# Q and K of two units by halves, and the end of the softmax as one lump for seven groups of heads, in a kernel of two attention layers

## The chip, the cores and the metric

The kernel runs on one core of a Trainium2 chip. The metric is the device time of one execution in microseconds (us), as the median of several runs. Inputs and outputs are in fp32, and each matrix product is made of three matmuls on fp32r parts of the numbers.

## The reference: two attention layers side by side

Two layers, A and B, have inputs of their own: x of 2048 positions by 1024, a weight for Q, K and V (1024 by 3072) and an output weight (1024 by 1024); 32 heads of 32. Their outputs stand side by side. In layer A a position sees 8 keys, each two positions apart; in layer B it sees the 256 keys up to itself.

```
# layer A
off = jnp.arange(8) * 2
idx = pos[:, None] - off[None, :]
logits = jnp.einsum("bhsd,bhswd->bhsw", q, kg) * scale      # kg, vg: k, v gathered at idx
attn = _softmax(jnp.where(mask[None, None, :, :], logits, -1e9))
o = jnp.einsum("bhsw,bhswd->bhsd", attn, vg)
# layer B
mask = (idx[:, None] - idx[None, :] >= 0) & (idx[:, None] - idx[None, :] < 256)
# both: out = o.reshape(B, S, D) @ wo; concatenate([a, b], axis=-1)
```

## The kernel before

The work is cut into 8 units of 512 positions: units 0 to 3 are layer B, units 4 to 7 layer A. In layer A the even and the odd positions are two sequences of 1024, so that the 8 keys are neighbours, and units 4 and 5 are one of them, 6 and 7 the other. Each unit has 8 groups of four heads; group hg = 8 x unit + group, so 32 to 63 are layer A's.

A host-side planner writes the whole program. The list `plan` gives the pieces of matrix products in order: "qk" (Q and K of one group), "v", "vp" (values), "o" and "p" (output products). Each becomes a list of items, one item being three matmuls (`TERMS`: high by high, high by low, low by high) for one of eight slices k of the contraction. Beside this sequence, "g", stand the sequences of the attention: the scores and the values of each group. A model of all engines, `Clock` (`ck`), gives each item a time from which it may start; the loop at the end emits the item that the model says is ready first. `ck.defer(t, f)` puts a follow-up step into a list of later steps that is emitted, in order of modelled time, among the others. So the order in which the steps stand on an engine comes out of modelled times, and a change in one place can move others.

Weights and x come as raw fp32 by DMAs that GpSimd issues (L221). Each is split in two fp32r parts: the high part by a cast on ScalarE (L276) or VectorE (L279), the low part by a subtraction on VectorE (L282). The x of a unit comes in four DMAs of two slices each.

All matmuls stand at L324. PSUM has three banks in a ring for matrix products (tag g), four for scores (s), one for values (o). An item with k = 0 takes a bank; the copy that empties it gives it back. Q and K are emptied on ScalarE (L586, L591), values' projections by a copy into vbuf (L720), output products on VectorE (L902) or ScalarE (L925).

A group of layer A goes through `window`: 128 small matmuls for the scores of four heads, mask on VectorE (L1217), maximum (L1227), subtraction (L1229), exponential on ScalarE (L1233), sum (L1241) and reciprocal (L1243), then `scale` (L1247) and `turn`, a transpose (L1254), each deferred to the modelled end of the step before it; `spread` writes the result into the block-diagonal `wide` by eight copies on ScalarE (L1263, L1266). The values' matmuls (o<-wide,vbuf) follow, are copied out at L1336 and stored to DRAM through od. In units 4 to 7 the sums that VectorE makes of blocks of the weights and outputs for products with fewer multiplications stand at L1104 and L1136.

In the tables of the profile PE is TensorE, PEld its weight loads, DVE VectorE, ACT ScalarE, POOL GpSimd and SP SyncE.

Of the kernel before, what the change touches and what calls it, by code (L numbers as in the profile page):

```python
# [16 lines left out]
NK = 8  # L17
# [13 lines left out]
EXTRA, EACH = 246, 5.2  # L31
P_LATE = 1.5
PAIRED = 50
VPARTS = ((0,4),(4,2),(6,2))
V_SLOTS = {0:0,5:1,7:2}
O_SLOTS = {2: (0, 1), 3: (2, 3), 4: (4, 5), 5: (6, 7)}
# [255 lines left out]
def kernel(ctx, tc, xs, wqk, wv, wo, outs, units):  # L292
# [3 lines left out]
    U = len(units)  # L296
    DU = sum(u[2] for u in units)
# [18 lines left out]
    ck = Clock()  # L316
# [98 lines left out]
    for p in plan:  # L415
# [7 lines left out]
        elif p[0] == "v":  # L423
            s0, n = VPARTS[p[2]]
            for i, g in enumerate((0, 1) if n == 2 else (0, 1, 2, 3, 0)):
# [97 lines left out]
    pfree = [0.0]  # L523
    vbuf = [const.tile([P, 6, n * P], F32, name=f"vbuf{i}") for i, (_, n) in enumerate(VPARTS)]
    vpart = {s0 + i: (p, i * P) for p, (s0, n) in enumerate(VPARTS) for i in range(n)}
    tails = const.tile([P, NG, 8], F32, name="tails")
# [37 lines left out]
    def latest(*ts):  # L564
        return None if any(t is None for t in ts) else max(ts)
# [162 lines left out]
    def v_items(u, part):  # L728
# [4 lines left out]
        h = {"w": {}}  # L733
        s0, ng = VPARTS[part]
        wide = ng == 4
# [330 lines left out]
    def value_load(part):  # L1066

        u = VPAIR + 1
        s0, n = VPARTS[part]
        if (u, part) in done["v"] or len(done["vd"]) < 4 or \  # L1070
# [94 lines left out]
    def x_items(u):  # L1165
        xt[u], xready[u] = [], []

        def run(g):
            a, b = st.get(where["x", u, g])
            xt[u] += a  # L1170
            xready[u] += b

        return [[(lambda: 0.0, lambda g=g: run(g), 0.0, lambda: None)] for g in range(4)]


    def window(u, s):
# [4 lines left out]
        hg = u * NG + s  # L1181
# [6 lines left out]
        def p16():  # L1188
            return band[buf][:, :1024].rearrange("p (i c) -> p i c", c=64)[:, :, 24:]
# [3 lines left out]
        h = {}  # L1193

        def scores_ready():
            if last_dense + 1 < hg < PAIRED and hg - 1 not in done["p"]:
                return None
            return latest(rs.empty(), done["stack"].get((u, s)), done["p"][hg - 1] + P_LATE if last_dense + 1 < hg < PAIRED else 0.0,
                          done["clear"].get(buf) if hg - 2 <= last_dense else done["o"].get(hg - 2))
# [25 lines left out]
        def top():  # L1225
            nm = small.tile([P, 16], F32, tag="nm", name="nm")
            nc.vector.tensor_reduce(nm, p16(), axis=mybir.AxisListType.X, op=ALU.max)  # L1227
            ck.use("dve", 0.855, ck.now)
            nc.vector.tensor_tensor(p16(), p16(), nm[:, :, None].to_broadcast([P, 16, 40]), op=ALU.subtract)  # L1229
            e = ck.use("dve", 0.86, ck.now, port=True)  # L1230

            def expo():
                nc.scalar.activation(p16(), p16(), AF.Exp)  # L1233
                e2 = ck.use("act", 0.645, e)
                ck.defer(e2 - 0.1, lambda: total(e2))

            ck.defer(e - 0.1, expo)

        def total(e):
            sm = small.tile([P, 16], F32, tag="sm", name="sm")  # L1240
            nc.vector.tensor_reduce(sm, p16(), axis=mybir.AxisListType.X, op=ALU.add)  # L1241
            ck.use("dve", 0.855, e)
            nc.vector.reciprocal(sm, sm)  # L1243
            e = ck.use("dve", 0.285, ck.now)

            def scale():
                nc.vector.tensor_tensor(p16(), p16(), sm[:, :, None].to_broadcast([P, 16, 40]), op=ALU.mult)  # L1247
                e = ck.use("dve", 0.86, ck.now, port=True)
                ck.defer(e - 0.1, turn)

            ck.defer(e - 0.1, scale)

        def turn():
            nc.vector.transpose(band[buf][:, 1024:], band[buf][:, :1024])  # L1254
# [14 lines left out]
        def values_ready():  # L1269
            if hg + 1 < PAIRED and hg + 1 not in done["scores"]:  # L1270
                return None
            return latest(done["v"].get((u, vp)), h.get("p") and h["p"] + P_LATE, ro.when())
# [14 lines left out]

        return [Item(scores_ready, scores, CW, 256 + (16 * len(kbs) if hg < PAIRED else 0))], [Item(values_ready, values, C3 + 0.9, 16 * len(kbs))]

# [260 lines left out]
    def fill(at, n):  # L1550

        def run():
            mm(ps, idle[:, :P], idle, start=True, stop=True)

        def after(last):
            if last:
                rs.give(bank, ck.now + ck.SEM)

        return [(lambda: 0.0, run, CG, lambda i=i: after(at == FILL[-1][0] and i == n - 1)) for i in range(n)]
# [10 lines left out]
    for p in plan:  # L1570
        if not marks and p[1:] == (DU, 2) and p[0] == "qk":
            marks.append(len(gemm))
        if len(marks) == 1 and p[0] == "p":
            marks.append(len(gemm))
        if p[0] == "qk":
            new = qk_items(p[1], p[2])
            if p == ("qk", 0, 0):
                q, k, x = new[:NK], new[NK:], x_items(0)
                f = dict(FILL)
                new = x[0] + sum([q[i:i + 1] + fill(i + 1, f.get(i + 1, 0)) for i in range(4)], [])  # L1580
                for i in (1, 2, 3):
                    new[new.index(q[2 * i]) if i < 2 else len(new):0] = x[i]
                    if i == 1:
                        new += k[:4]
                    else:
                        new += q[2 * i:2 * i + 2] + k[2 * i:2 * i + 2]
            if p[1:] == (0, NG - 1):
                x1 = x1 or x_items(1)
                for g in range(3, FIRST_X - 1, -1):
                    new[NK + 2 * g - 2:NK + 2 * g - 2] = x1[g]  # L1590
            gemm += new
        elif p[0] == "v":
            new = v_items(p[1], p[2])
            if p[1:] == (0, 2) and FIRST_X:
                x1 = x_items(1)
                for g in range(FIRST_X - 1, -1, -1):
                    new[X1_AT[g]:X1_AT[g]] = x1[g]
            elif V_SLOTS.get(NG - 1) == p[2] and 0 < p[1] < U - 1:
                m = 2 * VPARTS[p[2]][1]
                for g, x in reversed(list(enumerate(x_items(p[1] + 1)))):  # L1600
                    new[m * g + XAT:m * g + XAT] = x
            gemm += new
        elif p[0] == "o":
            gemm += o_items(p[1], p[2])
        elif p[0] == "p":
            gemm += product(p[1], p[2])
        elif p[0] == "vp":
            new = value_product(p[2])
            if VP_AT.get((p[1], NG - 1)) == p[2:] and p[1] + 1 < U:
                for g, x in reversed(list(enumerate(x_items(p[1] + 1)))):  # L1610
                    new[4 * g + XAT:4 * g + XAT] = x
            gemm += new
# [87 lines left out]
```

## The time and profile before

| | |
|---|---|
| median of 3 runs | 1789.3 us (1788.56 to 1789.42) |
| profiled execution | 1788.09 us, span 1786.4 us |
| granted TensorE clock | 1.000 |
| PE busy | 1768.4 us (99%) |
| DVE busy | 1295.5 us (73%) |
| ACT busy | 936.9 us (52%) |
| POOL busy | 412.8 us (23%) |
| instructions | 38443 |

The span runs from the first to the last instruction of the profiled execution; its device time is 1.7 us longer. The busy share of an engine is an average over the program. Rows of the timeline give the start, the busy time, the engine, the line, the operation with output <- input, the number of instructions in the row, and in brackets the idle time ahead of it and what ended it.

### The profile page before, as it was taken

The numbers are of one execution on the slowest core, as the hardware profiler recorded it, in microseconds if no ns is written. First come the engines' busy times: TensorE is split into PE (matmuls) and PEld (weight loads), VectorE is DVE, ScalarE is ACT, GpSimd is POOL, SyncE is SP. The second block draws the span as 40 slices with busy tenths as digits, with TensorE's granted clock in tenths as the row PEclk, the third lists the DMA queues.
The fourth block names the chain that finished last, engine by engine and source line by source line (L and its number), as shares of the span: only waits on it lengthen the run. The fifth ranks groups of instructions, "written<-read, shape, count | busy, mean of one in ns | idle before, by whom it ended". The sixth has DMA issues, their size and how long they took to land.

```text
span 1786.4 us, 38443 instructions
## 1 busy us (share of the span) xinstructions
PE 1768.4 (99%) x14496; PEld 1440.2 (81%) x14496; DVE 1295.5 (73%) x2881; ACT 936.9 (52%) x2332; POOL 412.8 (23%) x962
## 2 busy tenths in 40 slices
PE   9999999999999999999999999999999999999999
PEld 7787778888777888778788788878888887877887
DVE  6777876768867769867669546566577868767866
ACT  5565566555656565655654524444354546455442
POOL 3322324222333233242323410110011101001210
PEclk9999999999999999999999999999999999999999
DMA  8354664645645556555556255656576758948984
GB/s 256 106 151 136 187 167 137 163 135 152 186 142 154 154 127 173 150 148 156 133 142 186 72 181 180 210 193 209 175 219 197 233 169 290 303 151 271 310 319 144
DMA packets 154793, 324.57 MB, mean 182 GB/s; under 512 B 18032, under 2 KB 58992, under 8 KB 154608
## 3 DMA queue, kind: packets, MB, share of 16 engines
q0 software_dynamic: 45792, 166.74, 30.3%
q1 hardware_dynamic: 98736, 137.02, 26.9%
q10 hardware_dynamic: 10080, 18.35, 2.8%
q8 instruction: 115, 1.88, 0.4%
q14 instruction: 70, 0.57, 0.1%
HBM read 201.33 MB, written 53.48 MB: 143 GB/s over the span
## 4 chain that ended last, share of the span: by engine, by line
PE 92%; DVE 2%; DMA 2%; ACT 2%; issue 1%; SPq 0%; ACTq 0%; DVEq 0%; POOLq 0%
PE g L324 72%; PE s L324 13%; PE o L324 7%; DMA raw<-xs 1%; DVE w L282 1%; ACT s L1403 0%; DMA raw<-sd 0%; DMA pbuf<-nat 0%; DMA raw<-wqk 0%; DVE x L282 0%; ACT w L276 0%; DMA raw<-sx 0%; DMA qst<-nat 0%; ACT wide L1263 0%; ACT x L276 0%
## 5 line engine op out<-in xcount | busy, mean ns | idle before, releaser
L324 PE MATMUL g<-x,w 128*128 128x512 f32 x3552 | 875.8, 393 | 2.9 <-ACT x L276 1.0
L324 PEld LDWEIGHTS g<-x,w 128*128 128x128 f32 x3552 | 655.9, 188 | 131.7 <-issue 6.6
L282 DVE TENSOR_TENSOR w<-raw,w 128x512 fp32r<-128x512 f32 x510 | 334.3, 697 | 53.5 <-ACT w L276 47.2
L1398 DVE CUSTOM_DVE_ANT_0 s<-s,mask_d 128x384 f32<-128x384 f32 (+2 forms) x512 | 261.8, 554 | 98.4 <-PE s L324 98.1
L1403 ACT ACTIVATE s<-s,nm 128x384 f32<-128x384 f32 (+2 forms) x512 | 274.3, 537 | 109.9 <-DVE nm L1398 103.3
L324 PE MATMUL g<-w,x 128*128 128x256 f32 (+1 forms) x1728 | 306.9, 327 | 0.9 <-DVE w L282 0.7
L1462 POOL TENSOR_SCALAR_AFFINE_SELECT pbuf<-pbuf 128x128 f32<-128x128 f32 (+1 forms) x605 | 220.1, 392 | 315.7 <-ACT pbuf L1483 313.6
L324 PEld LDWEIGHTS g<-w,x 128*128 128x128 f32 x1728 | 255.3, 190 | 26.3 <-DVE w L282 2.2
L324 PE MATMUL g<-r,w 128*128 128x512 f32 x960 | 238.4, 393 | 0.5 <-DVE r L1362 0.5
L1483 ACT ACTIVATE pbuf<-s 128x384 f32<-128x384 f32 (+2 forms) x480 | 203.4, 504 | 65.3 <-PE s L324 63.5
L324 PEld LDWEIGHTS g<-r,w 128*128 128x128 f32 x960 | 177.2, 188 | 36.0 <-DVE r L1362 1.1
L221 POOL DMA_DIRECT2D raw<-wqk x126 | 68.4, 543 | 388.9 <-DVE w L282 265.2
L324 PEld LDWEIGHTS s<-qst,kst 128*128 128x128 f32 x704 | 113.5, 188 | 42.2 <-ACT s L1403 16.9
L324 PE MATMUL s<-kst,qst 96*128 96x384 f32 (+2 forms) x512 | 142.2, 342 | 0.9 <-ACT s L1403 0.7
L324 PE MATMUL s<-qst,kst 128*128 128x256 f32 (+2 forms) x704 | 137.0, 301 | 4.0 <-ACT s L1403 3.2
L279 DVE CAST w<-raw 128x1024 fp32r<-128x1024 f32 x176 | 121.3, 689 | 8.8 <-PE g L324 7.9
L324 PEld LDWEIGHTS s<-kst,qst 96*128 96x128 f32 x512 | 93.6, 189 | 26.2 <-issue 4.5
L276 ACT CAST w<-raw 128x1024 fp32r<-128x1024 f32 (+1 forms) x80 | 82.4, 1037 | 51.7 <-PE g L324 16.0
L1403 ACT ACTIVATION_READ_ACCUMULATOR s<-s,nm 128x1 f32 x512 | 105.3, 206 | 0.0
L1263 ACT COPY wide<-band 32x512 f32<-32x512 f32 x128 | 79.0, 617 | 30.3 <-DVE band L1254 28.8
L324 PE MATMUL o<-pbuf,vbuf 128*32 128x384 f32 (+2 forms) x1408 | 91.1, 388 | 0.0
L625 ACT ACTIVATE nat<-g 128x512 fp32r<-128x512 f32 x64 | 38.3, 598 | 97.7 <-PE g L324 87.1
(90 smaller groups left out, 1426.6 us busy)
## 6 DMA issues: line engine op xcount, KB each, us to landing
raw<-wqk POOLq DMA_DIRECT2D x126, 512.0 KB, 4.6
raw<-wv POOLq DMA_DIRECT2D x60, 512.0 KB, 4.8
qst<-nat SPq DMA_DIRECT2D x96, 256.0 KB, 4.2
kst<-nat SPq DMA_DIRECT2D x96, 256.0 KB, 5.5
raw<-wo POOLq DMA_DIRECT2D x44, 512.0 KB, 4.4
raw<-xs POOLq DMA_DIRECT2D x28, 512.0 KB, 4.5
kst<-halo SPq DMA_DIRECT2D x72, 128.0 KB, 4.5
pbuf<-nat SPq DMA_DIRECT2D x128, 65.0 KB, 3.2
```

The lines of the kernel that those rows point to most:

```text
L221: (self.nc.scalar if early else self.nc.gpsimd).dma_start(raw if len(ap.shape) == 2 else raw.rearrange("p (a b) -> p a b", a=2), ap)
L276: nc.scalar.copy(t[:, 0, :], raw)
L279: nc.vector.tensor_copy(t[:, 0, :], raw)
L282: nc.vector.tensor_tensor(t[:, 1, c:c + 512], raw[:, c:c + 512], t[:, 0, c:c + 512].bitcast(F32), op=ALU.subtract)
L324: nc.tensor.matmul(out, left, right, **k)
L625: nc.scalar.activation(hl[:, 0, :], ps, AF.Copy, scale=sc)
L1263: nc.scalar.copy(diag[r:r + 32, :, :, c:c + 32], turned[r:r + 32, :, :, 1, :])
L1398: nc.vector.tensor_tensor_reduce(ps[:, :n], ps[:, :n], mask[:, cut:full], scale=-1.0, scalar=BIG, op0=ALU.add, op1=ALU.min, accum_out=nm)
L1403: nc.scalar.activation(ps[:, :n], ps[:, :n], AF.Exp, bias=nm, scale=-1.0, accum_out=sm)
L1462: nc.gpsimd.affine_select(w, w, pattern=[[0, m], [step, n]], compare_op=ALU.is_ge, fill=0.0, base=base, channel_multiplier=chan)
L1483: nc.scalar.activation(w, ps[:, :pack * n].rearrange("p (j n) -> p j n", j=pack), AF.Exp)
```

## The change

Two things are changed. First, in `window` a new function `step` replaces the two `ck.defer` calls for `scale` and `turn`: for groups below `LUMPS` = 57 it defers as before, for groups 57 to 63 (unit 7 without its first group) it emits the step at once. Reciprocal, scale and transpose of these groups then stand directly behind each other on VectorE. Second, for the first group of units 5 and 6 the items of "qk" are put in another order: Q's slices 0 to 3, K's 0 to 3, Q's 4 to 7, K's 4 to 7. Before, all eight of Q came first. Q and K then have a bank open at the same time. (The first unit of layer A is unit 4, `DU`.) In the changed file the lines up to the new function stand one number lower down, those from `turn` on seven (L1247 becomes L1248, L1254 L1261).

```
--- before.py
+++ after.py
@@ -31,6 +31,7 @@
 EXTRA, EACH = 246, 5.2
 P_LATE = 1.5
 PAIRED = 50
+LUMPS = 57
 VPARTS = ((0,4),(4,2),(6,2))
 V_SLOTS = {0:0,5:1,7:2}
 O_SLOTS = {2: (0, 1), 3: (2, 3), 4: (4, 5), 5: (6, 7)}
@@ -1246,9 +1247,15 @@
             def scale():
                 nc.vector.tensor_tensor(p16(), p16(), sm[:, :, None].to_broadcast([P, 16, 40]), op=ALU.mult)
                 e = ck.use("dve", 0.86, ck.now, port=True)
-                ck.defer(e - 0.1, turn)
-
-            ck.defer(e - 0.1, scale)
+                step(e, turn)
+
+            step(e, scale)
+
+        def step(e, f):
+            if hg < LUMPS:
+                ck.defer(e - 0.1, f)
+            else:
+                f()
 
         def turn():
             nc.vector.transpose(band[buf][:, 1024:], band[buf][:, :1024])
@@ -1584,6 +1591,8 @@
                         new += k[:4]
                     else:
                         new += q[2 * i:2 * i + 2] + k[2 * i:2 * i + 2]
+            if DU < p[1] < U - 1 and p[2] == 0:
+                new = [new[c + i] for h in (0, NK // 2) for c in (0, NK) for i in range(h, h + NK // 2)]
             if p[1:] == (0, NG - 1):
                 x1 = x1 or x_items(1)
                 for g in range(3, FIRST_X - 1, -1):
```

Where instructions move, three places. In the rows, a name's number tells one buffer from another; "waits" names the semaphores that the instruction waits for. First TensorE at Q and K of unit 5: g_12557 is Q's bank, x_12418 to x_12532 are the eight slices of x, w_12414 and w_12488 the weights of Q and K. Before (the end of Q and the start of K, whose bank is g_12590):

```order
L324 MATMUL g_12557<-x_12529,w_12414 128x512 [waits Activation_49]
L324 MATMUL g_12557<-x_12529,w_12414 128x512 [waits DVE_49]
L324 MATMUL g_12557<-x_12529,w_12414 128x512
L324 MATMUL g_12557<-x_12532,w_12414 128x512 [waits Activation_49]
L324 MATMUL g_12557<-x_12532,w_12414 128x512 [waits DVE_49]
L324 MATMUL g_12557<-x_12532,w_12414 128x512
L324 MATMUL g_12590<-x_12418,w_12488 128x512 [waits Activation_49]
L324 MATMUL g_12590<-x_12418,w_12488 128x512 x2
L324 MATMUL g_12590<-x_12421,w_12488 128x512 x3
L324 MATMUL g_12590<-x_12454,w_12488 128x512 x3
L324 MATMUL g_12590<-x_12457,w_12488 128x512 x3
```

Now (K's bank is g_12574):

```order
L325 MATMUL g_12557<-x_12457,w_12414 128x512 [waits Activation_49]
L325 MATMUL g_12557<-x_12457,w_12414 128x512 [waits DVE_49]
L325 MATMUL g_12557<-x_12457,w_12414 128x512
L325 MATMUL g_12574<-x_12418,w_12488 128x512 [waits Activation_49]
L325 MATMUL g_12574<-x_12418,w_12488 128x512
L325 MATMUL g_12574<-x_12418,w_12488 128x512 [waits DVE_49]
L325 MATMUL g_12574<-x_12421,w_12488 128x512 x3
L325 MATMUL g_12574<-x_12454,w_12488 128x512 x3
L325 MATMUL g_12574<-x_12457,w_12488 128x512 x3
L325 MATMUL g_12557<-x_12492,w_12414 128x512
L325 MATMUL g_12557<-x_12492,w_12414 128x512 [waits DVE_49]
L325 MATMUL g_12557<-x_12492,w_12414 128x512
```

K's first four slices have moved ahead of Q's last four, and the matmuls of Q behind them have lost their wait for ScalarE, which stands at K's first matmul. In unit 6 the same move takes place.

Second, ScalarE at the same place: x_12529 and x_12532 are the last two slices of x, g_12402 and g_12424 the two banks of unit 4's last values. Before:

```order
L276 CAST x_12529<-raw_12523 128x512 [waits DMASW4_49,PE_49]
L276 CAST x_12532<-raw_12523 128x512 [waits PE_49]
L720 COPY vbuf2_129<-g_12402 128x512 [waits PE_49]
L720 COPY vbuf2_129<-g_12424 128x512 [waits PE_49]
L586 ACTIVATE nat_12588<-g_12557 128x512 [waits DMAHW4_49,DMAHW3_49,DMAHW5_49,DMAHW2_49,DMAHW6_49,DMAHW1_49,DMAHW7_49,DMAHW0_49,PE_49]
L1263 COPY wide_10858<-band_10856 32x16x32 [waits DVE_49]
```

Now:

```order
L277 CAST x_12529<-raw_12523 128x512 [waits DMASW4_49,PE_49]
L277 CAST x_12532<-raw_12523 128x512 [waits PE_49]
L721 COPY vbuf2_129<-g_12402 128x512 [waits PE_49]
L721 COPY vbuf2_129<-g_12424 128x512 [waits PE_49]
L277 CAST w_12586<-raw_12555 128x1024 [waits DMASW5_49,DVE_49]
L1270 COPY wide_10858<-band_10856 32x16x32 [waits DVE_49]
```

The casts and the two copies stand as they did; behind them the cast of a weight of V has come in from VectorE, and Q's L587 copy (L586 before) has moved behind the copies into wide.

Third, VectorE and ScalarE at the end of the softmax of group 62, whose buffer is band_10856. VectorE before, from the sum to the scale (the transpose stands seven rows further down):

```order
L1241 TENSOR_REDUCE sm_18594<-band_10856 128x16 [waits Activation_49]
L1243 RECIPROCAL sm_18594<-sm_18594 128x16 [waits DVE_49]
L282 TENSOR_TENSOR x_18622<-raw_18620,x_18622 128x512 [waits DMASW2_49,Activation_49]
L282 TENSOR_TENSOR x_18625<-raw_18620,x_18625 128x512 [waits Activation_49]
L282 TENSOR_TENSOR x_18630<-raw_18628,x_18630 128x512 [waits DMASW3_49,Activation_49]
L282 TENSOR_TENSOR x_18633<-raw_18628,x_18633 128x512 [waits PE_49,Activation_49]
L282 TENSOR_TENSOR w_18638<-raw_18636,w_18638 128x512 [waits DMASW4_49,PE_49,Activation_49]
L282 TENSOR_TENSOR w_18638<-raw_18636,w_18638 128x512
L1247 TENSOR_TENSOR band_10856<-band_10856,sm_18594 128x16x40 [waits DVE_49]
```

VectorE now:

```order
L1242 TENSOR_REDUCE sm_18584<-band_10856 128x16 [waits Activation_49]
L1244 RECIPROCAL sm_18584<-sm_18584 128x16 [waits DVE_49]
L1248 TENSOR_TENSOR band_10856<-band_10856,sm_18584 128x16x40 [waits DVE_49]
L1261 STREAM_TRANSPOSE band_10856<-band_10856 128x1024 [waits DVE_49]
L1137 TENSOR_TENSOR r_18425<-r_18425 128x512 [waits DMAHW7_49,DMAHW3_49]
L1137 TENSOR_TENSOR r_18425<-r_18424,r_18425 128x512 [waits DMAHW2_49,DVE_49]
L1137 TENSOR_TENSOR r_18424<-r_18425,r_18424 128x512 [waits DMAHW6_49,DVE_49]
L1137 TENSOR_TENSOR r_18424<-r_18424 128x512 [waits DVE_49]
L283 TENSOR_TENSOR x_18630<-raw_18628,x_18630 128x512 [waits DMASW2_49,Activation_49]
L283 TENSOR_TENSOR x_18633<-raw_18628,x_18633 128x512 [waits PE_49,Activation_49]
L283 TENSOR_TENSOR x_18638<-raw_18636,x_18638 128x512 [waits DMASW3_49,PE_49,Activation_49]
L283 TENSOR_TENSOR x_18641<-raw_18636,x_18641 128x512 [waits PE_49,Activation_49]
```

Scale and transpose have moved up to the reciprocal, and all four steps stand ahead of the four output sums (L1137). ScalarE before, at the two copies of a product (L925) and the casts for the next product; the copies into wide_10858 stand behind all of these:

```order
L925 COPY r_18587<-g_18568 128x512 [waits PE_49]
L925 COPY r_18587<-g_18597 128x512 [waits PE_49]
L276 CAST x_18622<-raw_18620 128x512 [waits DMASW2_49]
L276 CAST x_18625<-raw_18620 128x512
L276 CAST x_18630<-raw_18628 128x512 [waits DMASW3_49]
L276 CAST x_18633<-raw_18628 128x512
L276 CAST w_18638<-raw_18636 128x1024 [waits DMASW4_49]
L925 COPY r_18659<-g_18611 128x512 [waits PE_49]
L276 CAST w_18669<-raw_18646 128x1024 [waits DMASW5_49,Activation_49]
L925 COPY r_18659<-g_18662 128x512 [waits PE_49]
L276 CAST x_18785<-raw_18648 128x512 [waits DMASW6_49]
```

ScalarE now:

```order
L926 COPY r_18596<-g_18568 128x512 [waits PE_49]
L926 COPY r_18596<-g_18599 128x512 [waits PE_49]
L1270 COPY wide_10858<-band_10856 32x16x32 [waits DVE_49,Activation_49]
L1273 COPY wide_10858<-band_10856 32x16x8 [waits Activation_49]
L1270 COPY wide_10858<-band_10856 32x16x32 [waits Activation_49]
L1273 COPY wide_10858<-band_10856 32x16x8 [waits Activation_49]
L1270 COPY wide_10858<-band_10856 32x16x32 [waits Activation_49]
L1273 COPY wide_10858<-band_10856 32x16x8 [waits Activation_49]
L1270 COPY wide_10858<-band_10856 32x16x32 [waits Activation_49]
L1273 COPY wide_10858<-band_10856 32x16x8 [waits Activation_49]
L277 CAST x_18630<-raw_18628 128x512 [waits DMASW2_49]
L277 CAST x_18633<-raw_18628 128x512
```

The eight copies into wide stand ahead of the casts of x for that product. Around it, the values of group 62 stand 16 items earlier among TensorE's product items, and those of group 63 22 items earlier.

More of the change, by code (lines that the diff above doesn't have):

```diff
@@ L33 @@
 PAIRED = 50
+LUMPS = 57
 VPARTS = ((0,4),(4,2),(6,2))
@@ L1248, in scale, with step @@
                 e = ck.use("dve", 0.86, ck.now, port=True)
-                ck.defer(e - 0.1, turn)
-            ck.defer(e - 0.1, scale)
+                step(e, turn)
+            step(e, scale)
+        def step(e, f):
+            if hg < LUMPS:
+                ck.defer(e - 0.1, f)
+            else:
+                f()
         def turn():
@@ L1586 @@
                         new += q[2 * i:2 * i + 2] + k[2 * i:2 * i + 2]
+            if DU < p[1] < U - 1 and p[2] == 0:
+                new = [new[c + i] for h in (0, NK // 2) for c in (0, NK) for i in range(h, h + NK // 2)]
             if p[1:] == (0, NG - 1):
```

## The prediction

> **What bounds the kernel now.** I read the page first: busy times, chain, granted clock.
>
> ```profile
> PE 1768.4 (99%) x14496; PEld 1440.2 (81%) x14496; DVE 1295.5 (73%) x2881; ACT 936.9 (52%) x2332; POOL 412.8 (23%) x962
> ...
> PEclk9999999999999999999999999999999999999999
> ...
> PE 92%; DVE 2%; DMA 2%; ACT 2%; issue 1%; SPq 0%; ACTq 0%; DVEq 0%; POOLq 0%
> ```
>
> TensorE is busy for 1768.4 of 1786.4 us, so 18 us of the span is all that any reordering can win, and none of it comes from fewer matmuls, because the change removes none. The clock is full in every slice. The program is the same instruction by instruction up to Q and K of unit 5, which begin at 1143.75 us (below), so only what TensorE waits for after that point can go. The waits of TensorE from 1150 us to the end:
>
> ```profile
> PE g L324 <- DVE w L282: 0.7, 2, 0.5
> PE s L324 <- issue: 0.7, 1, 0.7
> PE s L324 <- DMA od<-r: 0.6, 1, 0.6
> PE g L324 <- DVE x L282: 0.5, 1, 0.5
> PE o L324 <- ACT wide L1266: 0.3, 1, 0.3
> PE g L324 <- DVE w L279: 0.2, 1, 0.2
> PE g L324 <- DVE pbuf L902: 0.2, 1, 0.2
> PE s L324 <- DMA pbuf<-nat: 0.2, 1, 0.2
> ```
>
> These sum to 3.4 us, and a wait of Q just before 1150 us comes on top (below). Windows of all engines show where the engines are full (the columns are length, then busy time of PE, PEld, DVE, ACT and POOL, granted clock, DMA share, GB/s):
>
> ```profile
> 1500.00:1525.00 25.00, 23.92 (x268) 18.76 (x271) 24.62 (x42) 15.41 (x29) 2.88 (x6) 1.00 0.97 325
> 1625.00:1650.00 25.00, 24.05 (x260) 19.39 (x259) 19.17 (x33) 15.23 (x27) 4.25 (x8) 1.00 1.01 352
> 1675.00:1775.00 100.00, 100.00 (x443) 82.81 (x442) 75.25 (x121) 38.70 (x55) 17.58 (x30) 1.00 0.75 263
> ```
>
> VectorE has 0.4 us of room in 1500 to 1525 us, and the last 100 us have no idle time on TensorE at all: an end of softmax that is ready earlier cannot shorten the tail.
>
> **Part 1, halves of Q and K in unit 5.** TensorE, then ScalarE, at that place:
>
> ```profile
> 1143.75 4.27 PE L324 MATMUL g<-x,w 128*128 128x512 f32 x18
> 1148.97 0.50 PE L324 MATMUL g<-x,w 128*128 128x512 f32 x1 [0.95 <-ACT x L276]
> 1149.97 6.90 PE L324 MATMUL g<-x,w 128*128 128x512 f32 x29 [0.51 <-DVE x L282]
> 1156.71 0.84 PE L324 MATMUL g<-w,x 128*128 128x512 f32 x3
> ```
>
> ```profile
> 1148.30 1.14 ACT L276 CAST x<-raw 128x512 fp32r<-128x512 f32 x2 [2.68 <-DMA raw<-xs]
> 1149.34 1.06 ACT L720 COPY vbuf<-g 128x512 f32<-128x512 f32 x2
> ```
>
> For the pace, Q and K of unit 6, which wait for nothing, with ScalarE beside them and the duration of one copy:
>
> ```profile
> 1321.09 11.07 PE L324 MATMUL g<-x,w 128*128 128x512 f32 x48
> 1331.99 1.52 PE L324 MATMUL g<-w,x 128*128 128x512 f32 x6
> ```
>
> ```profile
> 1322.98 1.14 ACT L276 CAST x<-raw 128x512 fp32r<-128x512 f32 x2 [2.57 <-DMA raw<-xs]
> 1324.02 1.06 ACT L720 COPY vbuf<-g 128x512 f32<-128x512 f32 x2
> ```
>
> ```profile
> L720 ACT COPY vbuf<-g x44: 576/587/595, 44.1 to 1324.5; 128x512 f32<-128x512 f32 x44
> ```
>
> 48 matmuls take 1331.99 - 1321.09 = 10.90 us, 0.227 each. In unit 5 Q's first 18 would be through at 1143.75 + 18 x 0.227 = 1147.84; the next starts at 1148.97, when the fourth piece of x has been cast, and the one after it not at 1149.20 but at 1149.97, when its low part is there. So Q loses 1.13 + 0.77 = 1.90 us. With K's first half put before Q's second, 24 matmuls stand ahead of that piece of x and not 18, and 6 more only reach 1149.20: nearly all of the cover that the change seeks is there.
>
> But K's first matmul now opens its bank after 12 matmuls and not after 24. The ring has three banks; the last part of unit 4's values holds two of them, Q has the third, and K gets the older of the two. It becomes free by the first L720 copy, and that stands on ScalarE behind the two casts of the fourth piece of x, which begin at 1148.30, when the DMA has landed. The new order says the same: K's first matmul waits for ScalarE, and the matmuls of Q on the fourth piece, behind it, no longer need a wait of their own for those casts. In before the same copy was ready long ahead of K. ScalarE's order is the same here, and so is that of the DMA issues.
>
> So: Q's first half ends at 1143.75 + 12 x 0.227 = 1146.47. The copy ends at 1149.34 + 0.59 = 1149.93, and TensorE follows within 0.1 us, as it did at 1148.97 the first cast of a pair that started at 1148.30 and took 1.14: 1149.99. The other 36 matmuls find all their inputs there and end at 1149.99 + 36 x 0.227 = 1158.16, against 1156.71. The 1.90 us go, 3.52 us come, together **+1.45 us**. Whatever stands behind this (values' weights, Q's evacuation, scores) is late by as much as TensorE is, so I count neither a gain nor a loss there; bounds for the step are -1.90 (the bank is free in time) and +1.6 (0.1 of slower hand-over).
>
> The Trainium skill, "PSUM — Partial Sum Buffer", section "Engine vs sequencer instructions", says that ScalarE's queue is strictly first in, first out, and that matmuls start in program order. The rows agree: the copy starts at 1149.34, just after the casts, though its matmuls had ended before 1143.75. By that rule neither the copy nor Q's second half can go around the wait, and the sum stays as it is.
>
> **Part 2, halves in unit 6.** K would be reached at 1321.09 + 12 x 0.227 = 1323.81. The first L720 copy ends at 1324.02 + 0.59 = 1324.61, again behind the last pieces' casts, and TensorE goes on at 1324.67: **+0.85 us**, and no wait was there to be won. Bounds 0 (the casts come 0.9 earlier against TensorE) and +0.85.
>
> **Part 3, the stretch from 1485 to 1527 us.** The new order moves scores and values by some products there. The four waits there (0.7 for issue, 0.3 for wide, 0.2 for w of L279, 0.2 for w of L282) are 1.4 us. All gone would be -1.4; all doubled with VectorE at 24.62 of 25 about +1.6. I take one more wait as long as the smallest for values, **+0.3**, since VectorE has no room to catch up.
>
> **Part 4, the lump.** By VectorE's order, groups 57, 59, 60 and 61 had scale and transpose side by side already; only 58, 62 and 63 change. Around 62 and 63, TensorE first, then VectorE, then ScalarE:
>
> ```profile
> 1634.18 0.23 PE L324 MATMUL s<-pbuf 32*32 32x40 f32 x2 [0.63 <-DMA od<-r]
> ...
> 1635.77 11.86 PE L324 MATMUL g<-x,w 128*128 128x512 f32 x51
> 1647.57 1.29 PE L324 MATMUL o<-wide,vbuf 128*32 128x8 f32 x40
> ...
> 1671.24 1.18 PE L324 MATMUL o<-wide,vbuf 128*32 128x8 f32 x40
> ```
>
> ```profile
> 1626.38 2.86 DVE L1136 TENSOR_TENSOR r<-r 128x512 f32<-128x512 f32 x4
> 1629.15 0.81 DVE L1241 TENSOR_REDUCE sm<-band 128x16 f32<-128x640 f32 x1
> 1630.00 0.25 DVE L1243 RECIPROCAL sm<-sm 128x16 f32<-128x16 f32 x1
> ...
> 1633.35 1.29 DVE L282 TENSOR_TENSOR w<-raw,w 128x512 fp32r<-128x512 f32 x2 [0.76 <-ACT w L276]
> 1634.56 0.82 DVE L1247 TENSOR_TENSOR band<-band,sm 128x640 f32<-128x640 f32 x1
> ...
> 1637.66 1.24 DVE L1254 STREAM_TRANSPOSE band<-band 128x1024 f32<-128x1024 f32 x1
> ```
>
> ```profile
> 1628.95 0.59 ACT L925 COPY r<-g 128x512 f32<-128x512 f32 x1 [2.13 <-PE g L324]
> 1629.44 2.18 ACT L276 CAST x<-raw 128x512 fp32r<-128x512 f32 x4
> 1632.27 1.05 ACT L276 CAST w<-raw 128x1024 fp32r<-128x1024 f32 x1 [0.65 <-DMA raw<-wo]
> ...
> 1643.93 0.61 ACT L1263 COPY wide<-band 32x512 f32<-32x512 f32 x1
> ...
> 1647.39 0.29 ACT L1266 COPY wide<-band 32x128 f32<-32x128 f32 x1
> ```
>
> The sum of group 62 stood behind the output sums at 1626.38 and now stands ahead of them: sum, reciprocal, scale, transpose are 0.81 + 0.25 + 0.82 + 1.24 = 3.12 us, so the transpose ends by 1629.50 instead of 1638.90. The eight copies (1643.93 to 1647.68, 3.75 us) follow the second L925 copy at once and end at 1633.3. The values of 62 now stand one product item (three matmuls, 0.68) behind the scores of 63, at 1635.77 + 0.68 = 1636.45: in time by 3 us. What they push back are the casts for the next product: x to 1633.3 + 2.18 = 1635.5, w to 1636.5, its low part to 1637.8. That product starts after two items and the values, at 1635.77 + 1.36 + 1.2 = 1638.3. So its cover is 0.5 us. Values of 63 come 22 items earlier, at about 1671.2 - 22 x 0.68 = 1656; they need nothing that VectorE's lump, some 3 us long, does not give by then. The same scores wait for a DMA (0.6 and 0.2), which the lump does not touch. Gain at most 1.0 (these two and the 0.2 at L902), loss at most 3.0 (3.75 less the cover of 0.5, rounded): I take **0**, the row that decides being the 1637.8 against 1638.3. Group 58 costs nothing: TensorE waits for nothing around it in the waits above.
>
> Sum: 1.45 + 0.85 + 0.3 + 0 = +2.6 us. The profiled execution took 1788.09 us around its span of 1786.4, and would take 1790.7; the median of the runs shown is 1789.3, 1.2 above it, and becomes **1791.9 us**. A measurement of this kernel can tell about 0.2% from no change, 3.6 us: below 1785.7 is faster, above 1792.9 slower.
>
> **The rivals.**
>
> Bank free, faster: if the fourth piece of x lands over 3.4 us earlier or the copy is not what K waits for, unit 5 gives -1.90 and unit 6 nothing. Against it: the casts and copies on ScalarE are back to back at 1148.30 and 1149.34. With the 1.4 of part 3 and the 1.0 of part 4 also won it is 1789.3 - 4.3 = 1785.0, chance 0.06; with the 1.9 alone 1787.4, chance 0.09.
>
> Copies ahead of casts, slower: the eight copies of 62 hold up ScalarE for 3.75 us, and the product's inputs behind them are late. It decides as soon as the transpose of 62 ends later than 1629.5 + 0.5 = 1630.0; then each further us is lost by TensorE, up to 3.0: 1791.9 + 3.0 = 1794.9. For it: the cover is 0.5 us against a chain of four engines. Chance 0.20.
>
> VectorE full, slower: the stretch of part 3 loses 1.6 rather than 0.3: 1793.2, chance 0.13 (0.10 of it beyond 1792.9).
>
> The clock, slower: the longest stop of TensorE after 1143 us is 1.1 us in before, with the clock at full; now it stops for 3.5 us. Should the clock then stand at half for as long as that stop, 3.5 us, half of these are lost, 1.75: 1791.9 + 1.75 = 1793.7, chance 0.05. The Trainium skill, "TensorE: Matmul & The Clock Gate", section "HAM oscillation — how this bites in real kernels", tells of such a fall after an idle gap of over about 3.4 us; no run here shows it so far.
>
> Nothing: three lumps of seven and two reordered pieces, whose waits cancel: 1789.3, chance 0.07.
>
> **How the numbers follow.** My own sum has 0.40, of which 0.33 below 1792.9 and 0.07 above. Faster: 0.06. Within 0.2%: 0.33 + 0.09 + 0.03 + 0.07 = 0.52. Slower: 0.07 + 0.20 + 0.10 + 0.05 = 0.42. The range goes from the case of 1787.4, less 0.2 for the spread of runs, to the copies' case with 1.1 of part 3 on top: 1787.2 to 1796.0. Outside lie the fully faster case and a few in a hundred above.
>
> **What would show it.** Right: in unit 5 TensorE runs 12 matmuls of Q, stops for about 3.5 us, released by ScalarE's L721 copy (a line lower in the changed file), then 36 without a stop, and starts the values at about 1158.2; in unit 6 a stop of about 0.85 us; values of 62 within 2 us after the scores of 63, no wait for x or w behind them; granted clock 1.00. Wrong: K's first matmul starts at 1146.5, or the copies stand ahead of the casts; a stop of over 1 us at the first product behind the values of 62; or a time under 1787.2, which would mean that the bank was never in the way.

## The result and the profile after

The changed kernel takes 1794.48 us (median of 7 runs) against 1788.56 us before (7 runs), 5.9 us more. The ratio is 1.0040, with a 95% interval of 1.0031 to 1.0049: slower by 0.4%. The profiled execution took 1794.15 us, its span is 1792.5 us against 1786.4, so 6.1 us are to be found.

What TensorE waited for from 1140 us on, in the changed kernel, the four largest rows (total, times, longest):

```profile
PE g L325 <- ACT vbuf L721: 3.0, 2, 2.4
PE g L325 <- DVE w L283: 2.0, 4, 0.7
PE g L325 <- DVE w L280: 1.5, 1, 1.5
PE g L325 <- DVE pbuf L903: 0.6, 1, 0.6
```

The first row is new: it is the copy that frees K's bank. The wait for x is gone, and the last three, all for VectorE, were 0.7, 0.2 and 0.2 us. TensorE's timeline in the changed kernel, at Q and K of unit 5, of unit 6, in the stretch around 1515 us, and at the end (start, busy time, instructions, idle time ahead):

```profile
1143.82 2.91 PE L325 MATMUL g<-x,w 128*128 128x512 f32 x12
1149.10 8.45 PE L325 MATMUL g<-x,w 128*128 128x512 f32 x36 [2.38 <-ACT vbuf L721]
1157.39 0.84 PE L325 MATMUL g<-w,x 128*128 128x512 f32 x3
...
1325.24 8.46 PE L325 MATMUL g<-x,w 128*128 128x512 f32 x36 [0.59 <-ACT vbuf L721]
1333.54 2.20 PE L325 MATMUL g<-w,x 128*128 128x512 f32 x9
...
1511.12 5.28 PE L325 MATMUL g<-x,w 128*128 128x512 f32 x22 [0.73 <-DVE w L283]
...
1519.29 0.49 PE L325 MATMUL g<-w,x 128*128 128x512 f32 x1 [1.53 <-DVE w L280]
...
1520.78 2.02 PE L325 MATMUL o<-wide,vbuf 128*32 128x136 f32 x32
...
1531.91 3.02 PE L325 MATMUL g<-w,x 128*128 128x512 f32 x12
...
1655.70 5.32 PE L325 MATMUL g<-x,w 128*128 128x512 f32 x22 [0.55 <-DVE w L283]
1661.58 0.93 PE L325 MATMUL g<-x,w 128*128 128x512 f32 x3 [0.56 <-DVE pbuf L903]
```

The matmul that starts at 1519.29, the values matmuls at 1520.78 and the 12 matmuls at 1531.91 are, in the kernel before, these:

```profile
1515.69 0.50 PE L324 MATMUL g<-w,x 128*128 128x512 f32 x1 [0.19 <-DVE w L279]
...
1517.08 1.12 PE L324 MATMUL o<-wide,vbuf 128*32 128x136 f32 x32
...
1526.78 3.02 PE L324 MATMUL g<-w,x 128*128 128x512 f32 x12
```

Read at the same instructions of both kernels, the lag grows like this: 1157.39 - 1156.71 = 0.7 us behind unit 5; 1333.54 - 1331.99 = 1.55 behind unit 6 (0.9 more); 1531.91 - 1526.78 = 5.1 behind the stretch (3.6 more); 6.1 at the end (1.0 more). So the stretch, in which no edited line runs, takes more than half.

A part of that is the clock. Windows of the changed kernel (length, busy times of the engines, granted clock, DMA share, GB/s):

```profile
1517.09:1520.50 3.41, 1.65 (x6) 0.69 (x5) 3.31 (x7) 3.24 (x8) 0.53 (x1) 1.00 1.07 352
1520.50:1523.91 3.41, 3.41 (x37) 2.38 (x36) 3.31 (x6) 1.15 (x3) 0.53 (x1) 0.50 0.95 243
```

Behind a window in which TensorE was busy for 1.65 of 3.41 us stands one of the same length at half clock; the 32 values matmuls in it, the row at 1520.78 above, take 2.02 us, where the same 32 take 1.12 in the kernel before. Half of 3.41 is 1.7 us. Read at the same instructions, the lag is 1519.29 - 1515.69 = 3.6 us ahead of this window and 5.1 behind it: the lowered clock makes 1.5 of the 3.6 us that the stretch adds, and the stops ahead of it 2.05 (3.6 less the 1.55 that were there before the stretch).

Why the stretch stops at all is on VectorE. The changed kernel:

```profile
1500.79 1.28 DVE L1011 TENSOR_TENSOR r<-g,r 128x512 f32<-128x512 f32 x2
1501.98 1.80 DVE L1105 TENSOR_TENSOR r<-r 128x256 f32<-128x256 f32 x4
1503.70 1.28 DVE L283 TENSOR_TENSOR x<-raw,x 128x512 fp32r<-128x512 f32 x2
...
1515.46 1.29 DVE L283 TENSOR_TENSOR w<-raw,w 128x512 fp32r<-128x512 f32 x2 [0.31 <-ACT w L277]
...
1518.55 0.69 DVE L280 CAST w<-raw 128x1024 fp32r<-128x1024 f32 x1
```

The kernel before:

```profile
1490.69 1.79 DVE L1104 TENSOR_TENSOR r<-r 128x256 f32<-128x256 f32 x4
...
1499.33 1.28 DVE L1010 TENSOR_TENSOR r<-g,r 128x512 f32<-128x512 f32 x2
1500.53 1.28 DVE L282 TENSOR_TENSOR x<-raw,x 128x512 fp32r<-128x512 f32 x2
...
1514.95 0.69 DVE L279 CAST w<-raw 128x1024 fp32r<-128x1024 f32 x1
```

The four sums have moved behind the start of x's low parts, into a stretch where VectorE hardly rests, and the cast for which TensorE waits comes 3.6 us later. Not all of this is the sums'. Ahead of them VectorE is already 1500.79 - 1499.33 = 1.5 us late, as TensorE is; behind them it is 1503.70 - 1500.53 = 3.2 late, so they add 1.7. The last 0.4 come with the stop of 0.31 us, a wait for the cast of a weight that starts on ScalarE at 1514.38, when the DMA raw<-tv has landed. That DMA is issued at 1505.28 (1502.11 in the kernel before), behind an earlier one at 1501.16 (1499.71): its distance to this one has grown by 1.7 us as well, and GpSimd waits there for x's low parts, which stand behind the sums.

### The profile page after: what moved, and what is told of

It is laid out like the page before. It is cut to its first block, busy times and chain, and to the rows that moved or that the text cites. A ratio compares the mean times of both kernels' runs of the same rounds, so it can differ in the third digit from the quotient of the medians.

```text
span 1792.5 us, 38451 instructions
## 1 busy us (share of the span) xinstructions
PE 1770.5 (99%) x14496; PEld 1440.7 (80%) x14496; DVE 1295.2 (72%) x2878; ACT 941.0 (52%) x2335; POOL 411.9 (23%) x962
## 3 DMA queue, kind: packets, MB, share of 16 engines
q8 instruction: 115, 1.88, 0.5%
## 4 chain that ended last, share of the span: by engine, by line
PE 92%; DMA 4%; ACT 2%; issue 2%; DVE 1%; POOL 0%; ACTq 0%; POOLq 0%; DVEq 0%
PE g L325 72%; PE s L325 13%; PE o L325 7%; DMA raw<-xs 1%; DMA raw<-tv 1%; DMA od<-r 1%; DVE w L283 1%; ACT s L1410 0%; DMA raw<-wqk 0%; ACT w L277 0%; ACT x L277 0%; DMA qst<-nat 0%; ACT wide L1270 0%; DVE qst L1445 0%; ACT pbuf L1490 0%
## 5 line engine op out<-in xcount | busy, mean ns | idle before, releaser
L277 ACT CAST w<-raw 128x1024 fp32r<-128x1024 f32 (+1 forms) x85 | 87.9, 1038 | 64.0 <-PE g L325 23.1
```

The lines of the kernel that those rows point to most:

```text
L277: nc.scalar.copy(t[:, 0, :], raw)
```

## The experiments

Each was timed against the kernel before, on the same chip. Ratios stand with their 95% interval; 0.1% is 1.8 us.

**The lump alone.** The reordering of Q and K is taken out.

```
-            if DU < p[1] < U - 1 and p[2] == 0:
+            if False and p[2] == 0:
```

> Q and K as in the kernel before, the lump for groups 57 to 63 kept. Theory A (each part costs what its stretch of the changed kernel's trace shows): about +1.1 us against before, all of it behind the values of group 62 and at the product items that follow. Theory B (the prediction's sum): 0, within 1 us. The mechanism that would be against both: -1 us, if the waits behind group 62 come only from what the halves delay. TensorE's order of scores and values is that of the changed kernel from group 58 on and that of before ahead of it.

Measured 1.0009 (1.0000 to 1.0018), medians 1789.48 against 1787.97. TensorE behind the values of group 62:

```profile
1648.87 5.28 PE L325 MATMUL g<-x,w 128*128 128x512 f32 x22 [0.55 <-DVE w L283]
1654.75 0.92 PE L325 MATMUL g<-x,w 128*128 128x512 f32 x3 [0.60 <-DVE pbuf L903]
```

The two stops of the changed kernel are here without any halves: they are the lump's. In time this is 0 to 3 us: it agrees with theory A's 1.1 and does not exclude 0.

**Halves alone.**

```
-LUMPS = 57
+LUMPS = 64
```

> The two reordered pieces kept, no lump. Theory A: +5.0 us against before (0.7 at unit 5, 0.9 at unit 6, 3.5 in the stretch from 1485 to 1530 us). Theory B: +2.6 us (1.45, 0.85, 0.3). If the time of the stretch came from the lump in some way, +1.6 to +2.3.

Measured 1.0028 (1.0019 to 1.0038), medians 1792.86 against 1787.97, 4.9 us more: theory A's 5.0, and not theory B's 2.6, which lies below the interval.

**Halves in unit 5 alone**, and **halves in unit 6 alone**, both without the lump.

```
-            if DU < p[1] < U - 1 and p[2] == 0:
+            if p[1] == 5 and p[2] == 0:        # the other: 6
```

> Q and K by halves in unit 5 alone, no lump. Both theories keep TensorE's order of scores and values as it was. Theory A: +0.7 us, the difference of a bank wait of 2.5 us and 1.9 us of waits for x. Theory B: +1.45 us (bank wait 3.5). If a delay of TensorE by 0.7 us is enough to upset the stretch from 1485 to 1530 us, +2 to +4.

> Q and K by halves in unit 6 alone, no lump. This alone brings all the moves of scores and values of groups 45 to 54. Theory A: +4.4 us (0.9 at unit 6, 3.5 in the stretch from 1485 to 1530 us, part of it at a lowered clock). Theory B: +1.15 us (0.85 and 0.3).

Unit 5: 1.0007 (0.9998 to 1.0016). Unit 6: 1.0020 (1.0011 to 1.0029), medians 1791.89 against 1787.97, 3.9 us. The parts add up: 0.07 + 0.20 + 0.09 = 0.36% against 0.40. Unit 6 is the bulk, and with it alone scores and values of groups 45 to 54 move, as in the changed kernel. Its profile has no lowered clock in the stretch, so the loss there does not need one. Unit 5 alone cannot be told from 0, nor does its time choose between theory A's 0.7 us and theory B's 1.45.

In unit 5 alone the clock shows again. TensorE's timeline and two windows of that kernel:

```profile
1148.83 10.08 PE L325 MATMUL g<-x,w 128*128 128x512 f32 x36 [2.14 <-ACT vbuf L721]
```

```profile
1145.62:1149.03 3.41, 1.27 (x6) 0.77 (x5) 3.31 (x7) 1.88 (x4) 1.46 (x2) 1.00 0.59 171
1149.03:1152.44 3.41, 3.41 (x9) 2.64 (x9) 3.41 (x6) 2.15 (x4) 0.72 (x1) 0.50 1.07 356
```

The 36 matmuls behind the stop take 10.08 us here, 8.45 in the changed kernel's profile, where the same stop (2.38 us) lowered nothing.

**Halves in unit 5, casts out of the copy's way.** The two high casts of the fourth piece of x go to VectorE; the planner's model is left as it is, so that nothing else moves.

```
-            nc.scalar.copy(t[:, 0, :], raw)
+            (nc.vector.tensor_copy if self.split in self.on_dve else nc.scalar.copy)(t[:, 0, :], raw)
...
+    st.on_dve = {where['x', u, 3] for u in (5,)}
```

> Q and K by halves in unit 5 alone, no lump, and the two high casts of the fourth piece of that unit's x on VectorE rather than ScalarE, so that the copy that frees K's bank no longer stands behind them; the order of scores and values is that of before. Theory A (K waits for a copy that stands behind casts): no stop of TensorE in Q and K of unit 5, and about -1.9 us against before, 3 us less than with halves alone. Rival (K's first matmul waits for the cast of its own weight or another step of ScalarE): a stop of over 1.5 us stays, and the time stays at +0.7 to +1.3.

Measured 0.9999 (0.9990 to 1.0007). TensorE:

```profile
1145.22 11.14 PE L326 MATMUL g<-x,w 128*128 128x512 f32 x48
...
1159.52 0.29 PE L326 MATMUL s<-pbuf 32*32 32x40 f32 x12 [1.34 <-issue]
```

The stop is gone, so K did wait for the copy behind the casts. But the 1.9 us did not come: 116 small matmuls later TensorE stands for 1.34 us with nothing shown that it waits for, a stop that was not there before, and a stop of that kind that ends at 1503.24 us is 1.34 long (0.66 in the kernel before, ending at 1501.76). Together TensorE stands 2.0 us longer at the two. (Q starts 1.5 us later in this profile than in the kernel before, because the clock was at 0.50 from 170.39 to 173.80 us in this execution, far ahead of the edit.)

**Halves in unit 6, casts out of the copy's way**: the same edit with unit 6.

> The same for unit 6 alone: halves, and the casts of the fourth piece of its x on VectorE; scores and values of groups 45 to 54 stand where halves in unit 6 put them. Theory A (the new order of scores and values costs the 2 us in the stretch from 1485 to 1530 us): no stop in unit 6, but the stretch still loses about 2 us more than before: +2. Rival (the stretch suffers from TensorE being 1.4 us late): 0 in both places, total 0.

Measured 1.0017 (1.0008 to 1.0026). TensorE:

```profile
1320.61 11.07 PE L326 MATMUL g<-x,w 128*128 128x512 f32 x48
...
1519.23 0.50 PE L326 MATMUL g<-w,x 128*128 128x512 f32 x1 [1.65 <-DVE w L281]
```

No stop in unit 6: TensorE is 0.5 us ahead of the kernel before there (1331.52 against 1331.99), and still 3.6 behind it after the stretch (1530.35 against 1526.78). So what costs is the new order, not the late arrival.

**Late without reordering.** The kernel before, with six matmuls more at the start of Q of unit 6.

```
                     h["w"], _ = st.get(where["qk", u, s, t])
+                    if (u, s, t) == (6, 0, 0):
+                        for _ in range(6):
+                            nc.tensor.matmul(h["ps"], h["w"][:, 0, :P], xt[u][0][:, 0, :], start=True, stop=True)
```

> The kernel before with six extra matmuls of 512 columns (1.4 us) at the start of Q of unit 6, and no change of order. Theory A: +1.4 us or a little less, since stops in the stretch absorb a part of it. Rival (lateness upsets the stretch): +3.5 us, as with halves in unit 6.

Measured 1.0002 (0.9994 to 1.0011), medians 1788.60 against 1788.53. This cannot be told from 0, nor from theory A's 1.4 us, but it excludes the rival's 3.5. In the profile TensorE is 2.3 us behind the kernel before after unit 6 (1334.28 against 1331.99), and 2.2 at the 12 matmuls behind the stretch (1528.98 against 1526.78): lateness alone does not grow there.

**The order without the sums.** Halves in unit 6, and the last set of four sums not computed.

```
-                nc.vector.tensor_tensor(*[t[:, c, :] for c in (to, x, y)], op=op)
+                if i < 23:
+                    nc.vector.tensor_tensor(*[t[:, c, :] for c in (to, x, y)], op=op)
```

> Halves in unit 6 alone, no lump, and the last set of four sums of weight blocks (1.8 us on VectorE, which the new order has moved to 1502 us, among the low parts of x) left out; its output then lacks those sums. Theory A (VectorE has no idle time from 1500 to 1518 us, and the sums that came in there push the last casts of weights back): about 1.8 us less than halves in unit 6 alone, +1.8 against before rather than +3.6. Rival (late DMAs of weights decide the stretch, or the other moves of scores and values): as halves in unit 6 alone, +3.6.

Measured 1.0008 (0.9999 to 1.0017). VectorE at the place of the sums and at the cast, and the 12 matmuls behind the stretch, without the sums:

```profile
1498.87 1.28 DVE L1011 TENSOR_TENSOR r<-g,r 128x512 f32<-128x512 f32 x2
1500.07 1.29 DVE L283 TENSOR_TENSOR x<-raw,x 128x512 fp32r<-128x512 f32 x2
...
1514.49 0.69 DVE L280 CAST w<-raw 128x1024 fp32r<-128x1024 f32 x1
...
1526.30 3.02 PE L325 MATMUL g<-w,x 128*128 128x512 f32 x12
```

And with them (halves in unit 6 alone):

```profile
1500.80 1.28 DVE L1011 TENSOR_TENSOR r<-g,r 128x512 f32<-128x512 f32 x2
...
1503.71 1.28 DVE L283 TENSOR_TENSOR x<-raw,x 128x512 fp32r<-128x512 f32 x2
...
1518.15 0.69 DVE L280 CAST w<-raw 128x1024 fp32r<-128x1024 f32 x1
...
1529.98 3.02 PE L325 MATMUL g<-w,x 128*128 128x512 f32 x12
```

Without the sums both come 3.7 us earlier and stand where they do in the kernel before. Of these, 1.9 us are there ahead of the sums already (1498.87 against 1500.80): in the execution without sums the fourth piece of x of unit 6 was cast early, from 1321.71 us rather than 1323.27, so that TensorE had no stop there and began the values' weights at 1331.70, 1.6 us earlier. From that row to the next another 1.7 us come in, close to the sums' own 1.8. So the profiles put 1.7 us on VectorE down to the sums, which is most of the 1.9 that the stretch adds with halves in unit 6 alone (a lag of 1.3 behind unit 6, 3.2 behind the stretch). In time, 0.12 of the 0.20% are gone, but the intervals of the two kernels overlap, so the time alone does not show it.

**The lump of group 62 alone**, and **of group 63 alone**, without halves.

```
-            if hg < LUMPS:
+            if hg != 62:        # the other: 63
```

> The lump for group 62 alone, no halves. Theory A (the 0.7 us behind the lump of group 63, and the 0.8 us for a bank that sums on VectorE keep): 0 to +0.4 us against before, no wait for the weight's low part near 1648 us. Rival (the eight copies of group 62 ahead of the casts of x): +1 or more, with a stop at the first product behind the values of 62.

> The lump for group 63 alone, no halves. Theory A: +0.7 to +1.2 us against before, with TensorE waiting about 0.7 us near 1648 us for the low part of a weight that stands behind sum, reciprocal, scale and transpose. Rival: 0 within 0.5 us.

Group 62: 0.9996 (0.9987 to 1.0004). Group 63: 1.0004 (0.9995 to 1.0013). Theory A blamed the lump of 63, and this falls: with 63 alone there is no stop near 1648 or 1655 us. VectorE there:

```profile
1648.73 1.29 DVE L283 TENSOR_TENSOR w<-raw,w 128x512 fp32r<-128x512 f32 x2 [1.65 <-ACT w L277]
...
1655.13 0.81 DVE L1242 TENSOR_REDUCE sm<-band 128x16 f32<-128x640 f32 x1
```

The weight's low part stands ahead of the sum of 63. Only where 62 is early too does 63's exponential come early, and its lump then lies ahead of that low part (changed kernel):

```profile
1651.84 0.81 DVE L1242 TENSOR_REDUCE sm<-band 128x16 f32<-128x640 f32 x1
...
1655.00 1.25 DVE L283 TENSOR_TENSOR w<-raw,w 128x512 fp32r<-128x512 f32 x2
```

So the stop needs both lumps, as far as these kernels show (with the lump of 57 to 63, that of 58 is there too, and was not tested by itself). The kernels of one lump have a time that cannot be told from before.

**Filling the stop.** Two kernels have halves in unit 5 alone, and multiply by a tile of zeros where TensorE would stand still: 40 matmuls of 128 columns, or ten of 512.

```
+                if (u, s, t, k) == (5, 0, 0, 3):
+                    for _ in range(10):
+                        nc.tensor.matmul(h["ps"], zero, xt[u][0][:, 0, :], start=False, stop=False)
```

> Halves in unit 5 alone, no lump, with 40 matmuls of zeros by zeros (128 columns, some 2.2 us) added to Q's sum where TensorE would stand still for K's bank. Theory A (a stop of over 2 us there can halve the clock for about 3 us): the clock is full behind it in the profile, and the time is +0.5 to +0.7 us against before, that is 0.5 to 1 less than halves alone, with less spread between runs. Rival (the lowered clock has another cause, or costs nothing in the end): as halves alone, +1.3, or more for the added matmuls.

> Halves in unit 5 alone, no lump, and ten matmuls of 512 columns with a weight of zeros (2.3 us) added to Q's sum where TensorE would stand still for K's bank; far fewer instructions than the 40 matmuls tried before. Theory A (the stop halves the clock for some 3 us): granted clock 1.00 behind it in the profile and +0.2 to +0.7 us against before. Rival (the dip has another cause, or is made up later): +1.3, as with halves alone.

With 40: 1.0081 (1.0068 to 1.0095). The matmuls took 4.58 us, not 2.2, and waits without a releaser appear in several later places (timeline, then TensorE's waits from 1140 us on):

```profile
1146.39 4.58 PE L694 MATMUL g<-zero 128*128 128x128 f32 x40
```

```profile
PE g L326 <- issue: 5.5, 6, 1.6
PE o L326 <- issue: 2.8, 2, 1.9
```

This kernel says nothing on the clock, but 40 short matmuls cost some 14 us, three times what they took. With ten, which took 2.46 us (timeline behind them, then a window):

```profile
1148.93 8.50 PE L326 MATMUL g<-x,w 128*128 128x512 f32 x36
```

```profile
1149.00:1152.00 3.00, 3.00 (x13) 2.46 (x14) 3.00 (x6) 1.90 (x3) 0.72 (x1) 1.00 0.98 359
```

The clock stays at 1.00 and the 36 matmuls take 8.50 us. Yet the time is 1.0012 (1.0003 to 1.0021), not less than the 1.0007 of halves alone. Of the three profiles with the stop of unit 5 (changed kernel, halves alone, halves in unit 5 alone) two have the lowered clock behind it, and neither of the two with the stop filled has it. That fits a dip that hangs on the stop, but it is a handful of executions. Whether the dip costs the end time is not shown by these kernels. In the list of runs a lower mean clock goes with a longer time: with halves in unit 5 alone six runs at 0.999 average 1790.0 us, five at 1.000 average 1787.9. A mean over a whole run does not say where its clock was low.

## Why the prediction was right, and where it was not

The direction held, and the result of 1794.5 lies in the range (1787.2 to 1796.0), partly by luck. The wait for K's bank, 2.3 of the 2.6 us forecast, was there, but it makes 1.6 of the 6.1 us in the profile. The rest came from the two parts that were given 0.3 and 0, and the range reached so far up for a case that did not occur, the copies of group 62 ahead of the casts. The forecast of 1791.9 was within 0.2% of no change, and the result is beyond that. By its steps:

Part 1 was right in kind: 12 matmuls, a stop released by the L721 copy, then 36 without a stop. Its size was 0.7 us rather than 1.45, because the casts of the fourth piece of x began at 1147.43 and not at 1148.30, and the copy with them:

```profile
1147.43 1.14 ACT L277 CAST x<-raw 128x512 fp32r<-128x512 f32 x2 [2.02 <-DMA raw<-xs]
1148.47 1.06 ACT L721 COPY vbuf<-g 128x512 f32<-128x512 f32 x2
```

They wait for a DMA, whose landing was taken from one execution. In unit 6 the same stop was 0.59, 0.96 and 1.24 us long in three profiles, and absent in the one without the sums. That the copy stands behind those casts was tested and holds. The rival of a free bank fell twice over: the bank was not free, and where it was made free, two stops without a releaser took 2.0 us more.

Part 2: 0.85 forecast, 0.9 in the profile. In time, taking the stop away (1.0017 against 1.0020) changes nothing that can be told; 0.9 us is less than these intervals can show.

Part 3 is the step that failed: +0.3, with a bound of +1.6, and it was 3.6: 1.7 for the sums, 0.4 for a late cast of a weight, 1.5 for the clock. The text had the reason in hand (VectorE with 0.4 us of room, and a rival, VectorE full, that gave the stretch 1.6), and it looked at how scores and values move but not at where the background sums land. Four sums of 1.8 us that move 11 us later, into a row of VectorE work without a gap, would have had to be added in full, and a lowered clock behind the stops on top.

Part 4: 0 forecast, 1.0 in the profile. The cover of 0.5 us that the product behind 62 had was enough; what was missed is the weight behind the lump of 63. The text asked what the values of 63 need of the lump, and not what the lump stands ahead of. (In time the lump's share, 1.0009, does not exclude 0.)

The clock, given 0.05, did come, but not where it was placed: in the changed kernel's profile behind several stops at 1515 us, and behind the stop of unit 5 only in the profiles of two other kernels with the same halves. The Trainium skill, "TensorE: Matmul & The Clock Gate", section "HAM oscillation — how this bites in real kernels", puts it at idle gaps over about 3.4 us. The runs differ: a stop of 2.1 us, or one of 1.5 with others beside it, was enough. In the section "What's actually happening" that page of the Trainium skill says that the clock is full again after a busy window of about 3.4 us; the 1149.03 to 1152.44 above, 3.41 us at 0.50, agrees.

Still open in part: what TensorE waits for at the stops without a releaser. They grow with added instructions (40 small matmuls) and with time won ahead of them. The traces hold a candidate, the DMA queue that the page lists as q8, instruction (115 packets, 1.88 MB). Its packets are blocks of 16 KB, about one in 10 us. In the profiles of all 14 kernels TensorE has 32 stops without a releaser behind 1140 us, and 30 of them end 0.9 to 1.5 us after such a block has landed; the stop of 1.34 us above ends at 1159.52, its block landed at 1158.26. So a wait for instructions is likely, but no experiment moved these blocks by themselves. No version was found that beats the kernel before: the two lowest, halves in unit 5 with the casts moved (0.9999) and the lump of 62 alone (0.9996), have intervals that hold 1.

## What to carry to other kernels

When an edit moves a planner's order, list all that moves on each engine that has a stretch without idle time, background work included, and charge what comes in there in full, however far from the edit, together with the buffers and DMAs that it holds back. Before two accumulations are opened at once, ask which instruction frees the second bank and what stands ahead of it in that engine's queue. A stop that is taken away is worth something only if the next stop does not grow by as much.

## What the runs showed of the hardware

The clock halves for 3.41 us (0.50 from 1149.03 to 1152.44, and from 1520.50 to 1523.91) behind windows in which TensorE was busy for 1.27 and 1.65 of 3.41 us, though the longest stop in them was 2.1 us. Each such fall in the middle of these profiles lasts 3.41 us. It does not follow from the busy time in one window alone. In the changed kernel's profile a window with 1.69 us left the clock at 1.00 in the window behind it (1148.45 to 1151.86). With halves in unit 6 and without the sums one with 2.07 us, most of its matmuls small ones, was followed by 0.50 (1636.82 to 1640.23). The two windows, the changed kernel's first, each counted back from the fall in its own profile in steps of 3.413 us, the length that the trace has for a fall:

```profile
1145.04:1148.45 3.41, 1.69 (x8) 1.07 (x6) 3.34 (x7) 1.39 (x3) 1.45 (x2) 1.00 0.69 187
...
1633.41:1636.82 3.41, 2.07 (x130) 1.74 (x130) 2.31 (x4) 2.58 (x3) 0.99 (x2) 1.00 1.04 359
```

Matmuls of 128 columns on this data type took 4.58 / 40 = 0.114 us each, where 512 columns took 0.227: a quarter of the columns for half of the time. Each had a weight load of its own, 40 loads in 4.66 us.
